# Batch 0's x in head pairs over two load queues, in a fused cross-attention and SiLU feed-forward kernel

## The chip, the core and the metric

The kernel runs on one core of a Trainium2 chip. The metric is the device time of one execution in microseconds (us). The core's engines run side by side and wait for one another through semaphores: TensorE (PE for matmuls, PEld for loading their weights), VectorE (DVE), ScalarE (ACT), GpSimd (POOL) and SyncE (SP). SP, ACT and POOL can issue DMA transfers, each on a queue of its own; in the profile SP's is q1, ACT's is q10 and POOL's is q0. Matmuls write to PSUM, which the kernel divides into eight banks; all else lies in SBUF.

## The reference

There are 8 batches, 8 heads, 512 tokens, 32 state rows and a head width of 64. Tokens attend to the state rows and state rows to the tokens; the two results are concatenated and go through a feed-forward layer with SiLU. Cut to what matters:

```python
scores = scale * np.matmul(x, state.transpose(0, 1, 3, 2))
a = np.exp(scores - scores.max(-1, keepdims=True))
a /= a.sum(-1, keepdims=True) + 1e-09
xread = np.matmul(a, state)
# sread: the same with the state as queries, and x as keys and values
attn = np.concatenate([xread, sread], axis=2)        # (8, 8, 544, 64)
x2 = attn.transpose(0, 2, 1, 3).reshape(8 * 544, 512)
h = x2 @ w_in                                        # (4352, 2048)
out = (h * (1.0 / (1.0 + np.exp(-h)))) @ w_out
```

The last line is `silu(h) @ w_out`; the softmax is over the 32 state rows for xread.

## The kernel before

All matmuls take bf16 operands and sum in f32. The kernel never forms xread. For each batch it multiplies the state with `w_in` once (`W1`, 256 rows by 2048), so that h comes from the softmax weights: `h = W1^T aT` (`emit_G1`, line 522), then SiLU on ACT (line 554) gives `g`, and `g` times `w_out` (`G2`, line 563) gives the output. A batch has 16 column tiles of h (`ft`, 128 columns each) and four tiles of 128 tokens (`tt`). State rows' results of all batches are worked off at the end (lines 543 and 585).

The order of the work is written out by hand: each engine runs its instructions in the order in which the program text emits them. A tile in a PSUM bank or SBUF buffer waits for the last reader of the one that held the place before.

What the change touches is the start of the program, batch 0, before the stream of G1 and G2 matmuls.

- **Loads.** ACT's queue loads batch 0's state (line 173), SP's queue loads x of batch 0 in two halves of four heads (line 179). POOL makes the identity matrix and then issues weight loads, which also cast to bf16 (lines 186 to 195). Line 177 is a small activation that makes ACT load its exp table.
- **Warming matmuls.** `keep_busy(n, ...)` runs n matmuls on zeros (line 165), 16 in all before the first real tile of h; their results are not used.
- **State.** The state's rows are cast on DVE, brought into transposed form by four matmuls (line 230), and copied into `stT` by DVE and ACT (lines 261 to 266).
- **x.** `cast_x` casts x to bf16 (lines 259, 260, 269, 270, 272: DVE, ACT and POOL share the two halves). `pe_transpose_x` transposes four heads (two pairs) at a time on TensorE (line 252), and DVE or ACT copies the result out of PSUM into `xT`. A pair is two heads, one above the other in the 128 partitions. POOL's cast at line 270 comes behind the loads that it issues.
- **Scores to weights.** `scores` (line 305) multiplies a pair's `xT` with `stT`; `exps` (line 319) takes exponentials on ACT; `norm` sums them on DVE (line 378), takes reciprocals (379) and multiplies (381) on POOL for the first four heads, and on DVE for the others. The results `an` are transposed on TensorE (line 397) into `aT`.
- **W1 of batch 0.** Its first 128 columns come from line 616, 384 more from lines 632 to 648, with matmuls on small tiles (line 468); the rest follows in the loop.
- **The first batch's loop** (lines 654 to 686). For each ft, `upto` emits tiles of h ahead of their use by `LEAD0[ft]`, `W0` says at which ft 512 further columns of batch 0's W1 are made, `W1_AT` at which ft a piece of batch 1's, and `T3` fits in the fourth token tile. `place_one_state` at ft 1 places batch 1's state.

In the profile all casts and copies stand under the lines of the helper `copy`: 157 on ACT, 159 on DVE and POOL. The tiles' names tell them apart: `x_rows<-x_f` is a cast of x, `xT<-ps_xt` a copy of transposed x, `aT<-ps_at` of transposed softmax weights, `W<-ps_w` of a piece of W1.

PSUM tiles of h rotate through two buffers, `psH`; `bank` hands out four others in turn.

Of the kernel before, what the change touches and what calls it, by code (L numbers as in the profile page):

```python
# [8 lines left out]
FP32 = mybir.dt.float32  # L9
# [33 lines left out]
def kernel(  # L43
# [105 lines left out]
    def load_w_in(f, n=512):  # L149
        nc.gpsimd.dma_start(w_in_sb[:, :, ds(f, n)], win_re[:, :, ds(f, n)])  # L150
# [4 lines left out]
    def copy(eng, dst, src):  # L155
        if eng is nc.scalar:
            nc.scalar.activation(dst, src, func=COPY, bias=0.0)  # L157
        else:
            eng.tensor_copy(dst, src)  # L159


    def keep_busy(n, pool, tag):
        ps = pool.tile([128, 512], FP32, tag=tag, name="ps_busy")
        for _ in range(n):
            nc.tensor.matmul(  # L165
                ps[:], busy[:, 0:128], busy[:], start=True, stop=True, skip_group_check=True
            )
# [7 lines left out]
        state[0].rearrange("h (m v) d -> (h m) (v d)", v=2),  # L175
    )
    nc.scalar.activation(warm[:], busy[:, 0:1], func=EXP, bias=0.0)
    for hg in range(2):
        nc.sync.dma_start(
            x_f[0][:, ds(4 * hg, 4), :, :],  # L180
            x[0, ds(4 * hg, 4)].rearrange("h (p c) d -> p h c d", p=128, c=4),
        )
    nc.vector.memset(stT[:, 0], 0.0)
    nc.vector.memset(stT[:, 1:8], 0.0)
    make_identity(nc, ident)
    load_w_in(0, 128)
    load_w_in(128, 384)
    load_w_out(0, 2)
# [32 lines left out]
            for v in range(2):  # L221
                copy(eng, by_n[:, :, 0:3:2, :, v], ps[ds(64 * v, 64), :, :, u, :])

    keep_busy(7, psH, "h1")
    copy(nc.vector, st0_n[:], st0_f[:])
    ps0 = bank([128, 4, 16, 2], FP32, "ps_st0")
    by_head = ident.rearrange("p (k u m) -> p k u m", u=2, m=16)
    for v in range(2):
        for u in range(2):
# [6 lines left out]
                tile_position=(0, 64 * u),  # L236
                skip_group_check=True,
            )
    keep_busy(2, psH, "h1")

# [3 lines left out]
    def pe_transpose_x(b, hg, nb=2, new=bank, engs=(nc.vector, nc.scalar), only=None):  # L244
        if b not in xT:
            xT[b] = xtpool.tile([128, 4, 4, 128], BF16, tag="xT", name=f"xT{b}")
        m = 4 // nb
        for u in range(nb) if only is None else only:
            ps = new([128, m, 2, 128], BF16, "ps_xt")
            for i in range(m):  # L250
                for j in range(2):
                    nc.tensor.transpose(  # L252
                        ps[:, i, j, :],
                        x_nat[b][:, m * u + i, 2 * hg + j, :],
                        ident[:],
                    )
            copy(engs[u], xT[b][:, ds(m * u, m), ds(2 * hg, 2), :], ps[:])

    cast_x(0, nc.vector, 0, 2, 0, 4)
    cast_x(0, nc.scalar, 2, 2, 0, 4)  # L260
    for u in range(2):
        copy(
            both[u],
            slots_of(0)[u].rearrange("p g (k n) -> p g k n", n=NS)[:, :, 0:3:2, :],
            ps0[ds(64 * u, 64)].rearrange("p (g k) m v -> p g k (m v)", g=2),
        )
    o_tags = ["o0", "o1"]
    new_o = lambda sh, dt, nm: psO.tile(sh, dt, tag=o_tags.pop(), name=nm)
    cast_x(0, nc.scalar, 2, 2, 4, 4)
    cast_x(0, nc.gpsimd, 0, 1, 4, 4)  # L270
    pe_transpose_x(0, 0, 2, new_o, (nc.vector, nc.vector))
    cast_x(0, nc.vector, 1, 1, 4, 4)

    st_x = pers.tile([128, 8, B, 4, 2, 2], BF16)

# [23 lines left out]
    def scores(b, hg, m=4, new=bank):  # L299
        sc_ps[hg] = []  # L300
        for c in range(4):
            if c % m == 0:
                sc_ps[hg].append(new([128, m, 4, NS], FP32, "ps_sc"))
            for j in range(2):
                nc.tensor.matmul(  # L305
                    sc_ps[hg][-1][:, c % m, ds(2 * j, 2), :],
                    xT[b][:, c, 2 * hg + j, :],
                    stT[:, b, 2 * hg + j, :, :],
                    start=True,
                    stop=True,  # L310
                    skip_group_check=True,
                )

    def exps(b, hg):
        e = epool.tile([128, 4, 4, NS], BF16, tag="exp", name="exp_nat")
        exp_nat[b, hg] = e
        n = 4 // len(sc_ps[hg])
        for i, ps in enumerate(sc_ps[hg]):
            nc.scalar.activation(e[:, ds(n * i, n)], ps[:], func=EXP, bias=0.0, scale=SCALE)  # L319
# [51 lines left out]
    def norm(b, hg, parts=((nc.gpsimd, 0, 4),), nr=4):  # L371
        e = exp_nat[b, hg]
        rs = att.tile([128, 4, 4, 1], FP32, tag="rs", name="rs")
        rc = att.tile([128, 4, 4, 1], FP32, tag="rc", name="rc")
        a = att.tile([128, 4, 4, NS], BF16, tag="an", name="an")
        an[b, hg] = a
        for c in range(0, 4, nr):
            nc.vector.tensor_reduce(rs[:, ds(c, nr)], e[:, ds(c, nr)], axis=AX, op=ADD)
        nc.vector.reciprocal(rc[:], rs[:])
        for eng, c, n in parts:  # L380
            eng.tensor_tensor(  # L381
                a[:, ds(c, n)],
                e[:, ds(c, n)],
                rc[:, ds(c, n)].to_broadcast([128, n, 4, NS]),
                op=MULT,
            )
        if hg == 0:
            aT[b] = att.tile([128, 2, 4, 128], BF16, tag="aT", name="aT")
# [95 lines left out]
    def w1_cols(b, cols, engs, new=bank):  # L484
        w1_out(b, cols, engs, w1_mms(b, cols, new))
# [31 lines left out]
    def g1_half(k, hg):  # L517
        b, ft = divmod(k, NFT)
        if hg == 0:
            pool, tag = (psA, "a1") if k == 1 else (psH, "h1")  # L520
            h_ps[k] = pool.tile([128, 512], FP32, tag=tag, name="h1")
        nc.tensor.matmul(  # L522
            h_ps[k][:],
            W1[b][:, hg, ds(128 * ft, 128)],
            aT[b][:, hg, :, :],
            start=(hg == 0),
            stop=(hg == 1),
            skip_group_check=True,
        )
# [73 lines left out]
            done[0] += 1  # L603

    new_h = lambda sh, dt, nm: psH.tile(sh, dt, tag="h1", name=nm)
    new_o = lambda sh, dt, nm: psO.tile(sh, dt, tag=o_tags.pop(), name=nm)
    keep_busy(1, psH, "h1")
    scores(0, 0)
    exps(0, 0)
    keep_busy(1, psH, "h1")  # L610
    pe_transpose_x(0, 1, 2, new_h, both)
    norm(0, 0)
    scores(0, 1, 2)
    exps(0, 1)
    norm(0, 1, ((nc.vector, 0, 4),), 2)
    w1_cols(0, [(0, 128)], (nc.scalar, nc.scalar))
    nc.scalar.activation(warm[:], busy[:, 0:1], func=SILU, bias=0.0)
    load_w_in(1024)
# [223 lines left out]
```

The softmax here doesn't subtract the row's maximum and nothing guards it: scores larger than these inputs give would overflow.

## Time and profile before

| | |
|---|---|
| median of 4 runs | 213.06 us (212.92 to 213.18) |
| time of the profiled execution | 212.92 us |
| its span, first to last instruction | 211.1 us |
| PE busy | 205.9 us, 97% |
| ACT, DVE, POOL busy | 139.2, 73.8 and 39.6 us |
| mean granted clock of TensorE | 0.997 |
| read from HBM, written | 17.43 MB, 8.91 MB |

The time and the span differ by 1.8 us that lie around the instructions. Engines overlap, so their busy times don't add up. PE's ends of matmuls are modelled: a new matmul starts before the one before it has ended, so where one group of equal matmuls is back to back, the spacing of the starts is its cost. Lines of the timeline read: start, length, engine, source line, operation, output and input with their shapes, how many in a row, and in brackets how long the engine had been idle and for whom it waited. In the views of the DMA traffic each queue stands with its packets, MB and the share of the 16 DMA engines that it took in that window.

### The profile page before, as it was taken

What the parts mean: (1) busy time and instruction counts of PE and PEld (TensorE: products, weight loads), DVE (VectorE), ACT (ScalarE), POOL (GpSimd) and SP (SyncE); (2) the same over time, 40 slices, a digit from 0 to 9 for tenths busy, and PEclk for the clock granted to TensorE, in tenths of its full rate; (3) what the DMA queues carried; (4) which work ended last, traced back from release to release, by engine and by line L of the source; (5) the groups of instructions that cost most, each with busy time, mean ns of one, the idle gap of its engine ahead of it and who ended that gap; (6) DMA issues with size and microseconds to landing.
All of it is one profiled execution on the core that took longest, in us unless ns stands there. A gap on an engine that the chain in (4) does not pass through costs nothing.

```text
span 211.1 us, 3864 instructions
## 1 busy us (share of the span) xinstructions
PE 205.9 (97%) x1575; PEld 96.9 (46%) x1575; DVE 73.8 (35%) x146; ACT 139.2 (66%) x244; POOL 39.6 (19%) x62
## 2 busy tenths in 40 slices
PE   7899999999999999999999999999999999999993
PEld 2443454455444444444444544444444444466653
DVE  3851267657741236113410653043412306100011
ACT  3865677899577867697569855996775166644410
POOL 8691313604220402021201302000200000000000
PEclk9999999999999999999999999999999999999998
DMA  5999999994749555546835628115321111011112
GB/s 190 204 201 207 288 260 350 231 277 159 108 123 267 169 127 126 135 163 106 226 93 175 109 67 200 50 50 102 83 66 43 62 60 53 0 50 50 53 50 99
DMA packets 42929, 28.65 MB, mean 136 GB/s; under 512 B 28064, under 2 KB 37792, under 8 KB 42912
## 3 DMA queue, kind: packets, MB, share of 16 engines
q1 hardware_dynamic: 36720, 20.65, 38.1%
q0 software_dynamic: 5904, 7.64, 17.4%
q8 instruction: 12, 0.20, 0.4%
q10 hardware_dynamic: 288, 0.13, 0.2%
q14 instruction: 5, 0.04, 0.1%
HBM read 17.43 MB, written 8.91 MB: 125 GB/s over the span
## 4 chain that ended last, share of the span: by engine, by line
PE 94%; DMA 3%; ACT 1%; DVE 1%; SPq 0%; issue 0%
PE o L563 51%; PE h L522 26%; PE ps_w L468 4%; PE h L543 3%; PE o_a L563 3%; DMA x_f<-in_x_dram 3%; PE o_part L585 2%; PE ps_sr L415 1%; PE ps_scT L331 1%; PE ps_busy L165 1%; PE ps_sc L305 1%; PE ps_at L397 0%; PE ps_xt L252 0%; DVE W L159 0%; ACT x_rows L157 0%; ACT exp_nat L319 0%
## 5 line engine op out<-in xcount | busy, mean ns | idle before, releaser
L563 PE MATMUL o<-w_out_sb,g 128*128 128x512 bf16 x496 | 131.8, 379 | 0.0
L554 ACT ACTIVATE g<-h 128x512 bf16<-128x512 f32 (+1 forms) x143 | 81.3, 573 | 35.3 <-PE h L522 21.2
L563 PEld LDWEIGHTS <-g 128*128 128x128 bf16 x528 | 50.2, 98 | 58.8 <-issue 3.9
L522 PE MATMUL h<-aT,W 128*128 128x512 bf16 x254 | 74.6, 379 | 0.1
L159 DVE COPY o_sb<-o 128x512 f32<-128x512 f32 x15 | 10.4, 691 | 89.6 <-PE o L563 86.1
L522 PEld LDWEIGHTS <-W 128*128 128x128 bf16 x254 | 24.5, 98 | 30.6 <-issue 1.2
L159 DVE CAST W<-ps_w 128x512 bf16<-128x512 f32 (+2 forms) x36 | 22.3, 659 | 23.7 <-PE ps_w L468 23.7
L157 ACT ACTIVATE W<-ps_w 128x512 bf16<-128x512 f32 (+1 forms) x32 | 16.3, 562 | 10.1 <-PE ps_w L468 10.1
L159 POOL CAST x_nat<-x_f 128x512 bf16<-128x512 f32 x24 | 14.2, 633 | 33.8 <-DMA x_f<-in_x_dram 33.8
L157 ACT ACTIVATE o_sb<-o 128x512 f32<-128x512 f32 x16 | 9.6, 597 | 14.3 <-PE o L563 11.8
L361 POOL TENSOR_TENSOR an<-e,rcn 128x512 bf16<-128x512 bf16 x5 | 7.6, 1519 | 50.3 <-DVE rcn L359 50.3
L468 PE MATMUL ps_w<-w_in_sb,stT 64*32 64x512 bf16 (+2 forms) x264 | 10.2, 374 | 0.0
L563 PE MATMUL o_a<-w_out_sb,g 128*128 128x512 bf16 x32 | 10.0, 379 | 0.0
L543 PE MATMUL h<-xmT,w_in_sb 128*128 128x256 bf16 x64 | 9.6, 273 | 0.0
L543 PEld LDWEIGHTS <-w_in_sb 128*128 128x128 bf16 x64 | 6.3, 98 | 3.9
L165 PE MATMUL ps_busy<-busy 128*128 128x512 bf16 x16 | 6.2, 506 | 1.2 <-DVE warm L172 1.2
L358 DVE TENSOR_REDUCE rs<-e 128x32 f32<-128x1024 bf16 x5 | 6.1, 1213 | 3.2 <-DMA e<-eT 3.2
L345 ACT ACTIVATE eT<-ps_scT 128x512 bf16<-128x512 f32 x10 | 5.4, 594 | 1.6 <-PE ps_scT L331 1.6
L784 ACT ACT_TABLE_LOAD x5 | 6.4, 1283 | 0.1
L381 POOL TENSOR_TENSOR an<-exp_nat,rc 128x512 bf16<-128x512 bf16 x3 | 3.1, 1049 | 14.6 <-ACT eT L345 9.4
L468 PEld LDWEIGHTS <-stT 64*32 64x32 bf16 x264 | 3.2, 90 | 5.5 <-issue 4.2
L766 ACT ACT_TABLE_LOAD x4 | 5.1, 1283 | 0.1
(76 smaller groups left out, 99.6 us busy)
## 6 DMA issues: line engine op xcount, KB each, us to landing
out_dram<-o_sb SPq DMA_DIRECT2D x33, 256.0 KB, 2.7
x_f<-in_x_dram SPq DMA_DIRECT2D x4, 1024.0 KB, 6.1
x_f<-in_x_dram POOLq DMA_DIRECT2D x2, 1024.0 KB, 12.1
w_in_sb<-in_moe_w_in_dram POOLq DMA_DIRECT2D x3, 512.0 KB, 10.4
x_f<-in_x_dram SPq DMA_DIRECT2D x2, 512.0 KB, 4.8
w_out_sb<-in_moe_w_out_dram POOLq DMA_DIRECT2D x4, 256.0 KB, 12.0
w_out_sb<-in_moe_w_out_dram POOLq DMA_DIRECT2D x2, 512.0 KB, 12.3
x_f<-in_x_dram POOLq DMA_DIRECT2D x2, 512.0 KB, 15.2
```

Source lines behind the costliest of these rows:

```text
L157: nc.scalar.activation(dst, src, func=COPY, bias=0.0)
L159: eng.tensor_copy(dst, src)
L165: nc.tensor.matmul(ps[:], busy[:, 0:128], busy[:], start=True, stop=True, skip_group_check=True)
L345: nc.scalar.activation(t[:, hg], scT_ps[hg][:], func=EXP, bias=0.0, scale=SCALE)
L358: nc.vector.tensor_reduce(rs[:], e2[b][:], axis=AX, op=ADD)
L361: eng.tensor_tensor(a[:, hg], e2[b][:, hg], rc[:, hg].to_broadcast([128, 4, 4, NS]), op=MULT)
L468: nc.tensor.matmul(pss[f, hg][ds(32 * s, 32), 0:n], stT[ds(r, 64), b, h // 2, s % 2, :], w_in_sb[ds(r, 64), h // 2, ds(f, n)], start=True, ...
L522: nc.tensor.matmul(h_ps[k][:], W1[b][:, hg, ds(128 * ft, 128)], aT[b][:, hg, :, :], start=(hg == 0), stop=(hg == 1), skip_group_check=True,)
L543: nc.tensor.matmul(ps[:, 0:256], w_in_sb[:, kt, ds(128 * ft, 128)], xmT[:, :, kt].rearrange("p t n b -> p t (n b)"), start=(kt == 0), stop ...
L554: nc.scalar.activation(g[:, 0:n], ps[:, 0:n], func=SILU, bias=0.0)
L563: nc.tensor.matmul(outs[tt][:], gt[b * NFT + ft][:, ds(128 * tt, 128)], w_out_sb[:, ft, :], start=(ft == 0), stop=(ft == NFT - 1), skip_gr ...
L784: nc.scalar.activation(warm[:], busy[:, 0:1], func=SILU, bias=0.0)
```

## The change

It has six parts.

1. x of batch 0 is loaded by four transfers of one pair (two heads, 256 KB) each: pairs 0 and 1 on SP's queue, pairs 2 and 3 on ACT's, after the activation that loads the exp table.
2. POOL writes the ones beside x in the first `x_rows` buffer (two memsets) before its first weight load, and no longer after the last ones.
3. Three warming matmuls less (7 to 6, 2 to 1, and one of those between the transposes).
4. Casts, transposes, scores and exponentials go by pairs. Casts: pair 0 on DVE, pair 1 on ACT, pair 2 on DVE, pair 3 half on ACT and half on POOL. All four copies of transposed x are DVE's. Scores of pairs 0 and 1 share a PSUM bank and one exponential; pairs 2 and 3 have one each.
5. The products of normalising are halves: both of the first four heads on POOL, and of the others one on DVE and one on POOL; all sums and reciprocals stand behind the last copy of xT on DVE.
6. In the first batch's loop, the first 512 columns of batch 1's W1 move from ft 4 to ft 2, beside those of batch 0; the lead at ft 1 is 3 and not 2; tiles 4 and 5 of h go to `bank` and not to `psH`.

```diff
-    for hg in range(2):
-        nc.sync.dma_start(
-            x_f[0][:, ds(4 * hg, 4), :, :],
-            x[0, ds(4 * hg, 4)].rearrange("h (p c) d -> p h c d", p=128, c=4),
-        )
+    for k in range(4):
+        load_x(0, 2 * k, 2, nc.sync if k < 2 else nc.scalar)
...
     make_identity(nc, ident)
+    ones_beside_x(0, nc.gpsimd)
     load_w_in(0, 128)
...
-    keep_busy(7, psH, "h1")
+    keep_busy(6, psH, "h1")
...
-    keep_busy(2, psH, "h1")
+    keep_busy(1, psH, "h1")
...
-    cast_x(0, nc.vector, 0, 2, 0, 4)
-    cast_x(0, nc.scalar, 2, 2, 0, 4)
+    cast_x(0, nc.vector, 0, 4, 0, 2)
...
-    cast_x(0, nc.scalar, 2, 2, 4, 4)
-    cast_x(0, nc.gpsimd, 0, 1, 4, 4)
-    pe_transpose_x(0, 0, 2, new_o, (nc.vector, nc.vector))
-    cast_x(0, nc.vector, 1, 1, 4, 4)
+    cast_x(0, nc.scalar, 0, 4, 2, 2)
+    cast_x(0, nc.gpsimd, 2, 2, 6, 2)
...
-            pool, tag = (psA, "a1") if k == 1 else (psH, "h1")
-            h_ps[k] = pool.tile([128, 512], FP32, tag=tag, name="h1")
+            if k == 1:
+                h_ps[k] = psA.tile([128, 512], FP32, tag="a1", name="h1")
+            else:
+                h_ps[k] = (bank if k in IN_BANKS else new_h)([128, 512], FP32, "h1")
...
+    IN_BANKS = (4, 5)
...
+    def pair_xT(k, new):
+        ps = new([128, 4, 128], BF16, "ps_xt")
+        for c in range(4):
+            nc.tensor.transpose(ps[:, c, :], x_nat[0][:, c, k, :], ident[:])
+        copy(nc.vector, xT[0][:, :, k, :], ps[:])
+
+    def pair_scores(k, ps):
+        for c in range(4):
+            nc.tensor.matmul(
+                ps[:, c],
+                xT[0][:, c, k, :],
+                stT[:, 0, k, :, :],
...
-    keep_busy(1, psH, "h1")
-    scores(0, 0)
-    exps(0, 0)
-    keep_busy(1, psH, "h1")
-    pe_transpose_x(0, 1, 2, new_h, both)
-    norm(0, 0)
-    scores(0, 1, 2)
-    exps(0, 1)
-    norm(0, 1, ((nc.vector, 0, 4),), 2)
+    ps_sc0 = bank([128, 4, 4, NS], FP32, "ps_sc")
+    pair_xT(0, new_o)
+    keep_busy(1, psH, "h1")
+    cast_x(0, nc.vector, 0, 4, 4, 2)
+    pair_xT(1, new_o)
+    pair_scores(0, ps_sc0[:, :, 0:2, :])
+    pair_xT(2, new_h)
+    pair_scores(1, ps_sc0[:, :, 2:4, :])
+    cast_x(0, nc.scalar, 0, 2, 6, 2)
+    nc.scalar.activation(e0[0][:], ps_sc0[:], func=EXP, bias=0.0, scale=SCALE)
+    for k in (2, 3):
+        if k == 3:
+            pair_xT(3, new_h)
+        ps = bank([128, 4, 2, NS], FP32, "ps_sc")
+        pair_scores(k, ps)
+        nc.scalar.activation(
+            e0[1][:, :, ds(2 * k - 4, 2), :], ps[:], func=EXP, bias=0.0, scale=SCALE
+        )
...
+    for hg in range(2):
...
+        for s, n in ((0, 4),) if hg == 0 else ((0, 2), (2, 2)):
+            nc.vector.tensor_reduce(
+                rs0[hg][:, :, ds(s, n)], e0[hg][:, :, ds(s, n), :], axis=AX, op=ADD
+            )
+        nc.vector.reciprocal(rc0[hg][:], rs0[hg][:])
+        for c in (0, 2):
+            (nc.vector if hg == 1 and c == 0 else nc.gpsimd).tensor_tensor(
+                an[0, hg][:, ds(c, 2)],
+                e0[hg][:, ds(c, 2)],
+                rc0[hg][:, ds(c, 2)].to_broadcast([128, 2, 4, NS]),
+                op=MULT,
+            )
...
-    for i in range(3):
+    for i in (1, 2):
         ones_beside_x(i, nc.gpsimd)
...
-    W1_AT = {4: 0, 6: 512}
-    LEAD0 = [2, 2, 2, 2, 2, 3, 2, 1, 3, 3, 2, 3]
+    W1_AT = {2: 0, 6: 512}
+    LEAD0 = [2, 3, 2, 2, 2, 3, 2, 1, 3, 3, 2, 3]
...
-        elif ft in W1_AT:
-            w1_cols(1, [(W1_AT[ft], 512)], both)
```

More of the change, by code (lines that the diff above doesn't have):

```diff
@@ L266 @@
         )
-    o_tags = ["o0", "o1"]
-    new_o = lambda sh, dt, nm: psO.tile(sh, dt, tag=o_tags.pop(), name=nm)
-    cast_x(0, nc.scalar, 2, 2, 4, 4)
-    cast_x(0, nc.gpsimd, 0, 1, 4, 4)
-    pe_transpose_x(0, 0, 2, new_o, (nc.vector, nc.vector))
-    cast_x(0, nc.vector, 1, 1, 4, 4)
+    cast_x(0, nc.scalar, 0, 4, 2, 2)
+    cast_x(0, nc.gpsimd, 2, 2, 6, 2)
     st_x = pers.tile([128, 8, B, 4, 2, 2], BF16)
@@ L605 @@
     new_h = lambda sh, dt, nm: psH.tile(sh, dt, tag="h1", name=nm)
+    IN_BANKS = (4, 5)
+    o_tags = ["o0", "o1"]
     new_o = lambda sh, dt, nm: psO.tile(sh, dt, tag=o_tags.pop(), name=nm)
-    keep_busy(1, psH, "h1")
-    scores(0, 0)
-    exps(0, 0)
-    keep_busy(1, psH, "h1")
-    pe_transpose_x(0, 1, 2, new_h, both)
-    norm(0, 0)
-    scores(0, 1, 2)
-    exps(0, 1)
-    norm(0, 1, ((nc.vector, 0, 4),), 2)
+    xT[0] = xtpool.tile([128, 4, 4, 128], BF16, tag="xT", name="xT0")
+    aT[0] = att.tile([128, 2, 4, 128], BF16, tag="aT", name="aT")
@@ new lines, in pair_xT @@
+    def pair_xT(k, new):
[9 more added lines that the diff above has]
+                stT[:, 0, k, :, :],
+                start=True,
+                stop=True,
+                skip_group_check=True,
+            )
@@ new lines @@
+    e0 = [epool.tile([128, 4, 4, NS], BF16, tag="exp", name="exp_nat") for _ in range(2)]
+    for hg in range(2):
+        exp_nat[0, hg] = e0[hg]
+    ps_sc0 = bank([128, 4, 4, NS], FP32, "ps_sc")
+    pair_xT(0, new_o)
+    keep_busy(1, psH, "h1")
+    cast_x(0, nc.vector, 0, 4, 4, 2)
[5 more added lines that the diff above has]
+    nc.scalar.activation(e0[0][:], ps_sc0[:], func=EXP, bias=0.0, scale=SCALE)
@@ new lines @@
+    for k in (2, 3):
[6 more added lines that the diff above has]
+        )
+    rs0, rc0, a0 = {}, {}, {}
+    for hg in range(2):
+        rs0[hg] = att.tile([128, 4, 4, 1], FP32, tag="rs", name="rs")
+        rc0[hg] = att.tile([128, 4, 4, 1], FP32, tag="rc", name="rc")
+        an[0, hg] = att.tile([128, 4, 4, NS], BF16, tag="an", name="an")
+        for s, n in ((0, 4),) if hg == 0 else ((0, 2), (2, 2)):
[9 more added lines that the diff above has]
+                op=MULT,
+            )
```

## The prediction

> **What bounds the kernel now.** I read the page first, then the chain of waits for the first 13 us, then the timeline of that stretch engine by engine, then DMA traffic in short windows.
>
> The page's busy line and the chain's split by engine:
>
> ```profile
> PE 205.9 (97%) x1575; PEld 96.9 (46%) x1575; DVE 73.8 (35%) x146; ACT 139.2 (66%) x244; POOL 39.6 (19%) x62
> PE 94%; DMA 3%; ACT 1%; DVE 1%; SPq 0%; issue 0%
> ```
>
> TensorE sets the time. The other 6% is the start, where batch 0 has to become scores before TensorE has real work. The chain there (start, length, what):
>
> ```profile
> 1.27 5.32 DMA x_f<-in_x_dram
> ...
> 6.61 0.63 ACT x_rows L157
> ...
> 7.27 0.60 ACT exp_nat L319
> 7.87 0.58 ACT xT L157
> ...
> 8.49 0.29 PE ps_sc L305 x4
> ...
> 11.39 0.49 PE h L506 x3
> 11.88 0.52 PE h L522 x2
> ```
>
> The second half of x lands at 6.59; cast, scores, exponentials, normalising and transposes follow, and the last matmul of the first h tile (third of the "x3", starts 0.11 apart) starts at 11.61. From there matmuls follow one another at 0.216 us for 512 columns; between 11.8 and 50 us the spacings hold only one stall near 0.22 us, one near 0.16 us and small ones. So the time moves by the shift of that 11.61, plus whatever the edits behind it save. The rows that I use for the shift:
>
> ```profile
> 5.83 0.75 POOL L153 DMA_DIRECT2D w_out_sb<-in_moe_w_out_dram  x1
> ...
> 6.64 0.40 POOL L159 CAST x_rows<-x_f 128x256 bf16<-128x256 f32 x1
> ...
> 7.61 0.42 DVE L159 COPY xT<-ps_xt 128x512 bf16<-128x512 bf16 x1 [0.42 <-PE ps_xt L252]
> ...
> 7.95 0.68 DVE L378 TENSOR_REDUCE rs<-exp_nat 128x16 f32<-128x512 bf16 x1
> ...
> 9.07 1.05 POOL L381 TENSOR_TENSOR an<-exp_nat,rc 128x512 bf16<-128x512 bf16 x1 [2.03 <-DVE rc L379]
> ```
>
> POOL casts only after its last early DMA issue. And the first reduction on DVE runs between copies of xT, while TensorE and ACT still work on the other heads.
>
> **The change part by part.**
>
> *Loads of x.* Two issues of 512 KB on SP become four of 256 KB: pairs 0 and 1 on SP, 2 and 3 on ACT. An issue takes 0.42 (ACT's state load) to 0.48 us (SP), so SP ends at 1.7 as now. ACT's two stand behind the first table load (1.20 to 2.48) in the program; later in this trace the records of ACT's sequencer have a semaphore wait of line 345 at 92.80, ahead of the table load at 93.41 that precedes it in the program, so I let the two issue at 1.2 and 1.7, before the first byte of x moves (2.0). Then both queues share. In the window 2.73 to 3.25:
>
> ```profile
> q1 hardware_dynamic: 119, 0.12, 66.3%
> q10 hardware_dynamic: 70, 0.03, 22.3%
> ```
>
> SP's q1 and ACT's q10 (state) went side by side. Packets of both up to 2.73, 3.25, 4.2 and 5.07 us are 129, 318, 670 and 1005, one KB each for x; q1 alone had 55, 174, 526 and 861. With equal turns from 2.73, SP has sent pair 0 (256 packets) at 129+2x201 = 531, that is at 3.83, and pair 1 (512) at 129+2x457 = 1043, at 5.2. The first half now reached 512 plus its completions at about 4.2 and landed at 5.09, 0.87 later. So pair 0 lands at 4.7, pair 1 at 6.1, pair 2 near 5.3, pair 3 at 6.4 to 6.6. Pair 1, worked second, comes third. Ends: 5.1 (pair 1 in the place of the first half now) and 6.59 (as late as the second half now). I take 6.1, from the shared window.
>
> A rule of the Trainium skill speaks against two queues: "DMA: Bandwidth & Descriptors", section "Issuing engines are not separate DMA queues", says that loads from several issuers interleave on the same 16 DMA engines and save only issue time. The rates of 372 and 383 GB/s from 3.25 to 5.07 on one queue agree. By the rule taken strictly pair 1 would gain nothing over 6.59, and the sum below would end at +1.1 in place of +0.6.
>
> *Weights later.* The two memsets of x_rows (0.33 and 0.13 us, overlapping to 0.30) move from 21.94 on POOL to before the first weight load: POOL's seven early issues and its cast move by 0.30 to 0.46; I take 0.4. No packet of q0 (weights) moves before 5.07, when x has 861 of 1056 packets out, so x gains little: 0 to 0.4 us at its last packets, and only pair 3 could use it. Weights lose 0 to 0.46; the first use is TensorE's at 8.71 (landed at 7.07) and 9.64 (landed at 9.32), both behind what moves more. Leaving POOL at 21.94 saves nothing: it waits for other things there.
>
> *The cast of pair 3 on POOL* (columns 2 and 3) now stands at 6.64+0.4 = 7.04 and ends at 7.44, whenever pair 3 lands before 7.0. Transposes of pair 3 cannot start before 7.5. That is a floor.
>
> *The staircase of pairs.* DVE and ACT run in program order. With pair 1 at 6.1: ACT casts it 6.12 to 6.75 (0.63). TensorE's transposes 6.80 to 6.97 (four, 0.056 apart); DVE's copy starts 0.26 after the last, as now (7.36 to 7.61), 7.23 to 7.65. Pair 2's transposes follow pair 0's scores, and its copy runs at 7.61 to 8.03; pair 2's scores at 8.09 to 8.18; only then pair 3's transposes (8.21 to 8.38), copy 8.64 to 9.06. Now one copy of xT runs on ACT beside DVE's; in the change all four are DVE's, and the third and fourth wait for each other through TensorE. DVE then does in a row what partly overlapped: reduction 0.68 and reciprocal 0.25 for the first four heads (to 9.94), two reductions of 0.42 and a reciprocal (to 10.96), a product of about 0.42 (half of 0.70 plus the fixed part). POOL does three half products, 0.53 each by half of 1.05: 10.10 to 11.16, and the last 11.16 to 11.70. DVE's product ends at 11.4, so POOL's is last. Transposes 11.75 and 11.81, copy 0.26 later for 0.29, last matmul of the first h at 12.42: +0.81. ACT (exponentials 0.60 and two of 0.38, W copies 0.44, table load 1.28) is through at about 11.6, in time. Hidden: the cast of pair 0 and of pair 2 (0.43 each) in DVE's wait for pair 1. The sequence moves one for one with pair 1: neutral at 5.3, +1.3 at 6.59, and not below about 0 because of POOL's floor (-0.25 if POOL's halves take less and DVE's path decides).
>
> *Fewer warming matmuls*, 16 to 13: they lie in waits, save nothing; whether the clock notices is a rival. Earlier start of the state's matmuls (one busy matmul less, 0.4 us at 4.28) is covered by the wait for pair 0.
>
> *Batch 1's first W1 piece from ft 4 to ft 2, lead and banks.* The rows show two visits to the small tiles now and one joined visit:
>
> ```profile
> 14.97 0.41 PE L468 MATMUL ps_w<-w_in_sb,stT 64*32 64x512 bf16 x8
> ...
> 18.03 0.41 PE L468 MATMUL ps_w<-w_in_sb,stT 64*32 64x512 bf16 x8
> ```
>
> Each entry and each exit costs 0.09 to 0.10 us over the column time (14.67 to 14.97, 15.00 to 15.32). One visit less saves 0.19. Its needs: batch 1's state placed by DVE (14.53 now, with the piece at about 15.2), both psH buffers free (SILU of the early fourth h ends some 0.6 us before), and the h of tiles 4 and 5 in other banks. The wait that could replace it costs 0 to 0.2; I keep -0.19.
>
> *Sum.* +0.81 - 0.19 = +0.62 on the profiled execution: 212.92 (span 211.1) to 213.54. The median of the runs is 0.14 higher, 213.06, so 213.7.
>
> **The rivals.**
>
> *Pairs land in their order* (ends at or below the time before). If ACT's loads wait behind the table load, they issue at 2.7 and 3.2, SP has the engines alone and pair 1 lands at about 5.1. For: they stand behind it in ACT's program. Against: the wait passed at 92.80. Pair 1 no longer decides; POOL's floor does: 0 to -0.25, with -0.19: -0.2 to -0.45, 212.6 to 212.9. It decides from pair 1 before about 5.3. Chance 0.22.
>
> *Weights become late.* Only if the start does not slip: w_in for tile 4 lands at 14.63 and is used at 14.97, w_out for ft 4 lands at 18.14 and is used at 18.37. A full 0.46 with an unmoved start gives 0.2 to 0.45 of stall, less 0.19: 213.1 to 213.3. Against: bytes that x leaves earlier are free for weights. Chance 0.08.
>
> *The clock comes later.* Warming matmuls start 0.43 apart up to 3.72 and 0.22 apart from 8.89:
>
> ```profile
> 1.19 3.17 PE L165 MATMUL ps_busy<-busy 128*128 128x512 bf16 x7 [1.19 <-DVE warm L172]
> ...
> 8.89 0.82 PE L165 MATMUL ps_busy<-busy 128*128 128x512 bf16 x3
> ```
>
> At half rate four transposes take 0.16 longer, three times in series, and the scores as much again; if it lasts past 11.6 each 512-column matmul loses 0.21. So +0.5 to +1.3 on top of +0.62: 214.2 to 215.0. For: TensorE's streaming up to 5.1 falls by about 0.4 us. Against: it still has six, four and one matmuls. The page "TensorE: Matmul & The Clock Gate" (Part 1) gives a free-running window of about 3.4 us for the switch; no row here shows the window. Chance 0.13.
>
> *x no faster and pair 1 last* is the late end of the forecast (+1.1, 214.2), and belongs to its range.
>
> **How the numbers follow.** Forecast 0.52, with its own range +0.25 to +1.1 (213.3 to 214.2); the rivals as above; 0.05 for none of these. Without the page's reading the late end stands from the row of 6.59. The range that leaves out 2 in 10 goes from 212.6, the in-order case, to 214.7 inside the late clock. A measurement of this kernel tells about 0.2% (0.43 us) from no change. Slower: 0.42 of the forecast, the clock's 0.13, 0.03 of the rest, 0.58. Faster: 0.10 of the in-order case and 0.02 of the rest, 0.12. Within: 0.30.
>
> **What would show it.** Pair 1's cast on ACT near 6.1 and not 5.1; POOL's cast near 7.0; DVE's four xT copies ending near 9.1 with three reductions after it; POOL's last product ending near 11.7; the last of the four first h matmuls near 12.4; one visit of 16 small-tile matmuls at ft 2 and none at ft 4. I am wrong if pair 1 lands by 5.3, if POOL's halves are much shorter than 0.53, if the transposes start 0.11 apart after 6 us, or if a stall appears at ft 2.

## The result and the profile after

| | before | after |
|---|---|---|
| median | 213.16 us (61 runs, 212.82 to 214.47) | 213.97 us (41 runs, 213.14 to 216.28) |
| ratio of the runs' means | | 1.0048, interval 1.0035 to 1.006 |
| profiled execution, its span | 212.92, 211.1 | 213.82, 212.1 |

The changed kernel is slower, by half a per cent in the mean and 0.4% in the median (ratios here are always of means), and its runs spread: 17 of the 41 lie at 213.50 or below, 8 between 213.79 and 214.32, 16 at 214.79 or above. Before, one run of 61 lies above 213.5. So there are two questions: what the typical loss is, and what makes the spread.

The page after the change, busy line and split of the chain:

```profile
PE 204.9 (97%) x1572; PEld 96.7 (46%) x1572; DVE 74.0 (35%) x147; ACT 138.5 (65%) x243; POOL 41.1 (19%) x64
PE 93%; DMA 4%; POOL 1%; DVE 1%; issue 0%; POOLq 0%
```

TensorE has a little less to do than before (205.9) and the span is longer, so the loss is waiting. The chain's share of the transfers went from 3% to 4%, and what is transferred has changed. The chain of waits up to 13 us (start, length, what):

```profile
1.31 0.26 POOL x_rows L115
1.56 0.05 POOL x_rows L118
1.61 0.87 POOL w_in_sb L150
2.48 8.41 DMA w_in_sb<-in_moe_w_in_dram
...
10.93 0.36 PE ps_w L461 x8
...
12.32 0.71 PE h L499 x4
```

Before, x headed this chain (5.32 us of transfer). Now it is the second piece of `w_in`, issued at 2.48 and landed at 10.89 (before 9.32). The last matmul of the first h tile (the fourth of "PE h L499") starts at 12.76, against 11.61: 1.15 us later. From that start to the end of the span it is 199.3 us, against 199.5 before: nearly the whole difference lies in the first 13 us, and the loop gives a little back.

The timeline of the same stretch (start, length, engine, line, operation, idle time before and for whom):

```profile
5.55 0.63 ACT L157 ACTIVATE x_rows<-x_f 128x512 bf16<-128x512 f32 x1 [0.16 <-DMA x_f<-in_x_dram]
...
6.75 0.40 POOL L159 CAST x_rows<-x_f 128x256 bf16<-128x256 f32 x1
...
8.05 0.42 DVE L159 COPY xT<-ps_xt 128x512 bf16<-128x512 bf16 x1 [0.61 <-PE ps_xt L610]
8.39 0.68 DVE L651 TENSOR_REDUCE rs<-exp_nat 128x16 f32<-128x512 bf16 x1
...
9.50 1.95 POOL L656 TENSOR_TENSOR an<-exp_nat,rc 128x256 bf16<-128x256 bf16 x3 [2.36 <-ACT W L157]
...
10.27 0.70 DVE L656 TENSOR_TENSOR an<-exp_nat,rc 128x256 bf16<-128x256 bf16 x1
...
10.93 0.36 PE L461 MATMUL ps_w<-w_in_sb,stT 64*32 64x384 bf16 x8 [1.03 <-DMA w_in_sb<-in_moe_w_in_dram]
...
16.23 0.63 PE L461 MATMUL ps_w<-w_in_sb,stT 64*32 64x512 bf16 x16
```

The reader sees two delays that lie beside each other. The staircase: DVE's fourth copy ends at 8.47, the reduction follows, and POOL's three half products end at 11.45, where its one product ended at 10.12. And the weights: TensorE has nothing to do from 9.90 and waits 1.03 us for the piece of `w_in`. The last line is the joined visit to the small tiles, 16 matmuls in a row.

The two delays can be told apart. In three later profiles of the same staircase in which no weights are waited for last (given below), the last h matmul starts 0.72 to 0.73 after POOL's last product ends (11.31 and 12.03, 11.85 and 12.58, 11.94 and 12.66). By the staircase alone it would be 11.45 + 0.72 = 12.17, 0.56 later than before; the remaining 0.59 is the weights'.

How x left the queues, in three windows one after the other, 2.73 to 3.50, 3.50 to 4.30 and 4.30 to 5.07 us (packets, MB, share of the 16 DMA engines):

```profile
q1 hardware_dynamic: 242, 0.24, 88.3%
q10 hardware_dynamic: 67, 0.03, 13.4%
...
q1 hardware_dynamic: 235, 0.23, 81.7%
q10 hardware_dynamic: 72, 0.07, 25.9%
...
q10 hardware_dynamic: 253, 0.24, 91.4%
q1 hardware_dynamic: 57, 0.04, 16.8%
```

SP's queue q1 had most of the engines until 4.3, then ACT's q10. The pairs landed at 4.37, 5.47, 5.88 and 6.61, in their order.

And how the weights moved. After 6.2 no packet of x is left in either kernel, and POOL's q0 is alone on the engines. From 6.2 to 7.2, 7.2 to 8.2 and 8.2 to 9.2 it moved 0.18, 0.20 and 0.20 MB before the change, and 0.15, 0.17 and 0.14 MB after it. The third of these stretches, first before, then after (a share above 100% means that packets overlap in time):

```profile
q0 software_dynamic: 224, 0.20, 125.0%
...
q0 software_dynamic: 173, 0.14, 118.1%
```

The 512 packets of the second piece of `w_in` (768 bytes each) begin at 5.81 before and 6.09 after, 0.28 later, but the last one begins at 8.91 and 10.52, 1.61 later. So most of its delay arises when x is already out, at a lower rate of the weights. Why the rate falls no run shows.

### The profile page after: what moved, and what is told of

It is laid out like the page before. It is cut to its first block, busy times and chain, and to the rows that moved or that the text cites. A ratio compares the mean times of both kernels' runs of the same rounds, so it can differ in the third digit from the quotient of the medians.

```text
span 212.1 us, 3868 instructions
## 1 busy us (share of the span) xinstructions
PE 204.9 (97%) x1572; PEld 96.7 (46%) x1572; DVE 74.0 (35%) x147; ACT 138.5 (65%) x243; POOL 41.1 (19%) x64
## 3 DMA queue, kind: packets, MB, share of 16 engines
HBM read 17.43 MB, written 8.91 MB: 124 GB/s over the span
## 4 chain that ended last, share of the span: by engine, by line
PE 93%; DMA 4%; POOL 1%; DVE 1%; issue 0%; POOLq 0%
PE o L558 51%; PE h L517 26%; DMA w_in_sb<-in_moe_w_in_dram 4%; PE ps_w L461 4%; PE h L538 3%; PE o_a L558 3%; PE o_part L580 2%; PE ps_sr L408 1%; PE ps_scT L324 1%; PE ps_sc L298 0%; PE ps_xt L250 0%; POOL w_in_sb L150 0%; PE h L499 0%; DVE W L159 0%; PE ps_at L390 0%; PE ps_busy L165 0%
## 5 line engine op out<-in xcount | busy, mean ns | idle before, releaser
L159 POOL CAST x_nat<-x_f 128x512 bf16<-128x512 f32 x24 | 14.8, 659 | 34.8 <-issue 34.0
L165 PE MATMUL ps_busy<-busy 128*128 128x512 bf16 x13 | 5.1, 510 | 1.2 <-DVE warm L172 1.2
L109 POOL DMA_DIRECT2D x_f<-in_x_dram x4 | 3.3, 841 | 9.3 <-DVE x_rows L159 7.0
```

The lines of the kernel that those rows point to most:

```text
L165: nc.tensor.matmul(ps[:], busy[:, 0:128], busy[:], start=True, stop=True, skip_group_check=True)
```

## The experiments

Three readings of the late weights were open at first: that the third queue (ACT's) is what slows them, that POOL's later start does, or that the order does in which loads of x and of weights are issued. Beside them stood the clock: fewer warming matmuls, and so a late full clock. In the expectations R stands for the third queue, P for POOL's later start, O for the order of issues and C for the clock. The runs came in three groups, each on one chip and beside runs of the kernel before (medians 213.0, 213.0 and 213.1).

### The ones back at their old place

```diff
-    ones_beside_x(0, nc.gpsimd)
     load_w_in(0, 128)
...
-    for i in (1, 2):
+    for i in range(3):
         ones_beside_x(i, nc.gpsimd)
```

> The changed kernel with the ones of the first x_rows buffer written where they were, after the last loads, so that POOL issues the first weight load 0.12 us earlier (at 1.43). Theory P: the 384 columns land near 9.4 and the median falls to 213.3. Theory R: nothing moves by more than 0.15 us; median 213.8 to 214.1.

Measured: 213.70 (213.06 to 214.88), ratio 1.0048 (1.003 to 1.0066): the same as the whole change, and not the 213.3 of theory P. Its profiled execution was the fastest, 213.06, with weights on time (the second piece of `w_in` landed at 9.36), so it stands for the best case and not for the median. Its timeline shows the staircase without the other delay:

```profile
7.02 0.40 POOL L159 CAST x_rows<-x_f 128x256 bf16<-128x256 f32 x1 [0.47 <-DMA x_f<-in_x_dram]
...
9.36 1.95 POOL L655 TENSOR_TENSOR an<-exp_nat,rc 128x256 bf16<-128x256 bf16 x3 [1.94 <-ACT W L157]
9.54 0.36 PE L460 MATMUL ps_w<-w_in_sb,stT 64*32 64x384 bf16 x8
...
11.48 0.81 PE L498 MATMUL h<-aT,W 128*128 128x256 bf16 x4
```

The last h matmul starts at 12.03, 0.72 after POOL's end at 11.31: the staircase costs 0.42, the loop gives 0.2 back, and the span is 211.3 against 211.1. The place of the ones is not what costs the median; POOL's first weight issue moves by 0.12 us only (1.43 to 1.55).

### All four pair loads on SP, and then the weights issued after them

```diff
-        load_x(0, 2 * k, 2, nc.sync if k < 2 else nc.scalar)
+        load_x(0, 2 * k, 2, nc.sync)
```

> The changed kernel, but all four pair loads of x on SP's queue. Theory R (the third queue in use is what makes the first weights late): the weight load of 128 columns lands near 7.2 us and that of 384 columns near 9.5 (8.86 and 10.89 in the changed kernel), TensorE does not wait for the latter, and the time falls to 213.0 to 213.4 with the runs close together. Theory P (weights are late because POOL starts them later): they land as late as in the changed kernel and the median stays near 214.0. Theory S (my staircase of pairs sets the start whatever the weights do): the last matmul of the first h still starts near 12.2 against 11.6 before, and about 0.4 us of loss remains, 213.5.

Measured: 217.07 (216.59 to 218.38), ratio 1.02 (1.0179 to 1.0222), much slower, with no x on ACT's queue at all. None of the forecasts (213.0 to 214.0) came near. Part of it is TensorE's clock, which in the profile was granted at half from 8.41 to 15.24 us. The chain of waits:

```profile
1.76 0.47 SPq L109
2.23 0.04 issue
2.27 7.97 DMA x_f<-in_x_dram
10.24 0.02 issue
10.26 0.42 ACT x_rows L157
```

Pairs 0 and 1 landed at 4.05 and 4.77, but pair 2 at 7.38 and pair 3 at 10.24. Their issues stand at 1.76 and 2.27, behind POOL's first weight issue at 1.55. The next kernel keeps SP's four loads and lets POOL write all three buffers of ones and a scratch tile first, so that the first weight issue comes at 3.05:

```diff
-    ones_beside_x(0, nc.gpsimd)
+    for i in range(3):
+        ones_beside_x(i, nc.gpsimd)
+    idle = pers.tile([128, 1024], BF16)
+    nc.gpsimd.memset(idle[:], 0.0)
     load_w_in(0, 128)
```

> As the first experiment (four pair loads on SP), but POOL writes all three buffers of ones and a scratch tile of 1024 columns before its first weight load, which so starts near 3.0 us, after SP's fourth issue at 2.27. Theory O (a load of x that is issued after the first weight load has begun shares the DMA engines with the weights and is stretched): the four pairs now land in order near 4.0, 4.8, 5.6 and 6.4, where they landed at 4.05, 4.77, 7.38 and 10.24; TensorE keeps the full clock from about 5 us on, and the time falls from 217 to 213.5 to 214.5, although all weights and POOL's cast of pair 3 come about 1.5 us later. Theory N (the third and fourth transfer on a queue are slow by themselves): pair 3 still lands after 8 us and the time stays above 216.

Measured: 215.72 (214.89 to 216.0). The pairs landed at 4.09, 4.80, 5.54 and 6.34, 0.7 to 0.8 apart, as theory O foresaw. Beside POOL's memsets nothing but the order of the issues differs, so these two profiles show it: a load of x issued after the first load of weights is stretched, by 1.8 us for pair 2 and 3.9 us for pair 3. The time fell by 1.35 us and missed the 213.5 to 214.5 expected: POOL's cast of pair 3 now stands behind its late issues, and the full clock, against the expectation, was lost again from 9.34 to 12.75 us. Its timeline:

```profile
6.36 0.42 ACT L157 ACTIVATE x_rows<-x_f 128x256 bf16<-128x256 f32 x1 [0.60 <-DMA x_f<-in_x_dram]
...
8.30 0.45 POOL L159 CAST x_rows<-x_f 128x256 bf16<-128x256 f32 x1
```

In the other kernels the first weight issue is POOL's at 1.43 or 1.55; two halves on SP are issued by 1.27, ACT's second pair at 1.77. What their profiles show:

| x of batch 0 | last x landed | second piece of `w_in` landed |
|---|---|---|
| two halves on SP (five kernels) | 6.44 to 6.59 | 9.32, 9.38, 9.68, 9.68, 9.76 |
| a half on each queue | 6.38 | 10.18 |
| pairs over two queues (six kernels) | 6.32 to 8.47 | 9.36, 10.16, 10.45, 10.66, 10.89, 11.04 |
| pairs on SP | 10.24 | 11.68 |

For x the table fits the order of the issues: what is issued ahead of the weights lands by 6.59, what is issued behind them lands as late as 8.47 or 10.24, though not always late. For the weights the order is not enough. With a half on each queue all of x is issued by 1.28, ahead of the weights, and still their second piece lands at 10.18, later than with any halves on SP. Theory R (ACT's queue in use) stays open for the weights, though it can't be the whole, as they land at 11.68 with SP alone and at 9.36 once with ACT's queue in use.

The rule that the prediction quoted from the Trainium skill, "DMA: Bandwidth & Descriptors", section "Issuing engines are not separate DMA queues", that loads of several issuers interleave on the same 16 engines, agrees with the rows: from 5.6 to 6.2 in the changed kernel's profile, POOL's queue (129.7%) and ACT's (18.0%) move packets side by side. Equal turns between the two queues of x, which the prediction had taken, are not in the rows.

### The loads alone in the kernel before

```diff
-    for hg in range(2):
-        nc.sync.dma_start(
...
+    for k in range(4):
+        load_x(0, 2 * k, 2, nc.sync if k < 2 else nc.scalar)
```

> The kernel before with nothing changed but the loads of batch 0's x: four pair loads, two on SP and two on ACT. Theory R: weights land late here too (9.8 to 10.9 for the 384 columns), TensorE waits for them, and the time goes to 213.4 to 214.2 with a wide spread. Theory P: weights land as before (9.3), time 213.1, within 0.1%. If the first half (pairs 0 and 1, both on SP) lands earlier than 5.09, the casts of the first four heads start earlier.

Measured: 213.94 (213.63 to 216.14), ratio 1.0057 (1.0035 to 1.0079). The new loads alone, with the old order of work, cost what the whole change costs. Theory R's numbers came out, but by theory O the weights would be late here too, so the run doesn't tell the two apart. The profiled execution was the slowest (216.14), with pair 3 at 8.47, `w_in` at 11.04, and the clock lost (below).

### The edit of the loop alone

```diff
-    W1_AT = {4: 0, 6: 512}
-    LEAD0 = [2, 2, 2, 2, 2, 3, 2, 1, 3, 3, 2, 3]
+    W1_AT = {2: 0, 6: 512}
+    LEAD0 = [2, 3, 2, 2, 2, 3, 2, 1, 3, 3, 2, 3]
```

(with tiles 4 and 5 of h in `bank`, as in the change)

> The kernel before with the loop's edit alone (batch 1's first W1 piece at ft 2, lead 3 at ft 1, tiles 4 and 5 of h in other banks). My step says one visit to the small tiles less, -0.19 us: ratio 0.9991, about 212.85 where before is 213.05, and no new wait at ft 2. The rival is a wait in its place: ratio 1.000 or above.

Measured: 212.82 (212.6 to 213.07), ratio 0.9993 (0.9984 to 1.0001): 0.15 less in the mean, 0.19 in the median. That is the gain foreseen, at the edge of what can be measured, and it is the lowest median of all kernels here.

### Two halves with the new order of work

In the first, x is loaded in halves on SP as before; in the second, one half on SP and one on ACT.

```diff
-    for k in range(4):
-        load_x(0, 2 * k, 2, nc.sync if k < 2 else nc.scalar)
+    for hg in range(2):
+        load_x(0, 4 * hg, 4, nc.sync)
```

> The changed kernel with the loads of x as before (two halves on SP); casts by pairs, later ones, fewer warming matmuls and the loop's edit stay. Theory O: both halves are issued before the weights (by 1.75), land at 5.1 and 6.6, and the runs lie within 0.6 us of one another; what is left is the staircase (pair 1 at 5.1; last copy of xT ends near 8.3, last matmul of the first h at 12.0 against 11.61) less 0.19 for the loop: 213.2 to 213.4. Theory P or C (weights' start, warming): spread up to 215 as in the changed kernel.

```diff
+    for hg in range(2):
+        load_x(0, 4 * hg, 4, (nc.sync, nc.scalar)[hg])
```

> The changed kernel with x in two halves, one on SP (heads 0 to 3, issued at 0.74) and one on ACT (issued at 1.27). Theory O: both issues precede the first weight load at 1.55, so x lands by 6.6 and the time is as with two halves on SP, 213.2 to 213.5, close together. Theory R (a third queue in use is the cause): weights late, spread as in the changed kernel, median near 214.0.

Measured: 215.49 (214.54 to 215.54) and 215.47 (214.56 to 215.62), ratio 1.0108 for both (1.0092 to 1.0124). The expectation of a small loss fell. With SP's halves the loads were as wanted, x at 5.02 and 6.46, `w_in` at 9.38; with a half on each queue x landed at 4.93 and 6.38, and `w_in` at 10.18. What cost the time is in TensorE's timeline of the first:

```profile
5.60 0.61 PE L610 MATMUL ps_xt<-ident,x_rows 128*128 128x128 bf16 x4 [0.60 <-DVE x_rows L159]
...
8.73 0.61 PE L610 MATMUL ps_xt<-ident,x_rows 128*128 128x128 bf16 x4
...
13.10 0.86 PE L390 MATMUL ps_at<-ident,an 128*128 128x128 bf16 x8
```

The changed kernel's profile has for the same four transposes of pair 0:

```profile
4.96 0.40 PE L610 MATMUL ps_xt<-ident,x_rows 128*128 128x128 bf16 x4
```

They take 0.61 in the one and 0.40 in the other (starts 0.107 apart and 0.056). TensorE ran at half speed up to 13.6 us; the records of the granted clock begin only there. (The view's column for the clock shows 1.00 before the first grant, and the mean clock of a run leaves that time out; the spacing of the matmuls tells.) So theory C came to the fore: the spread is the clock's.

The clock's records, in every profile, are cut in steps of 3.413 us: the changed kernel's full clock lasts 61 of them, the kernel before's 60, that of the halves 59, and in the run of the loads alone one step full and one half come first. So I took TensorE's busy time in the steps before and after each grant (ahead of the first grant there is no record, and the steps are counted back from it). Halves on SP, grant at 13.61:

```profile
3.37:6.78 3.41, 2.59 (x13) 1.00 1.18 290
6.78:10.20 3.42, 2.66 (x33) 1.00 1.26 198
10.20:13.61 3.41, 3.07 (x27) 1.00 1.27 204
```

The loads alone in the kernel before, granted at 7.19, half from 10.60 to 14.01, then full:

```profile
3.78:7.19 3.41, 3.41 (x21) 1.00 1.10 233
7.19:10.60 3.41, 1.55 (x24) 1.00 1.25 188
10.60:14.01 3.41, 3.41 (x29) 0.50 1.27 203
```

The two steps nearest to the limit, one of the half on each queue, not followed by a grant, and one of the weights behind SP's four loads, followed by one:

```profile
2.88:6.29 3.41, 2.79 (x13) 1.00 1.16 318
...
9.34:12.75 3.41, 2.80 (x24) 0.50 1.25 192
```

(The columns are the stretch, its length, PE's busy time as the view models it with the number of matmuls, the clock, the share of the DMA engines and GB/s.) In the 14 profiles of all kernels the clock was granted after every step with 2.80 us busy or more (lowest 2.80, 2.83, 2.90), not granted after steps of 2.79, 2.66, 2.61, 2.59 and 1.10, taken back after 1.55, 1.60 and 1.64, and kept after 1.97 and more. Busy times hold modelled ends of matmuls, so the limit is about 2.8 us here and no sharper. The page "TensorE: Matmul & The Clock Gate" of the Trainium skill (Part 1) describes a free-running activity window of about 3.4 us; these steps agree with it.

### The waits of TensorE filled

Theory C was put to the test by filling gaps with warming matmuls and taking them out where they were.

```diff
-    keep_busy(6, psH, "h1")
+    keep_busy(7, psH, "h1")
...
-    keep_busy(1, psH, "h1")
+    keep_busy(2, psH, "h1")
...
     pair_xT(0, new_o)
-    keep_busy(1, psH, "h1")
+    keep_busy(2, psH, "h1")
...
             pair_xT(3, new_h)
+            keep_busy(2, psH, "h1")
```

> The changed kernel with five warming matmuls more, all of them in stretches where TensorE waits: 7 and 2 at the start as before the change, 2 and not 1 after the transposes of pair 0, 2 between the transposes and the scores of pair 3. Theory C (clock): the profiles show full clock granted and taken back in steps of 3.413 us, and the changed kernel leaves TensorE idle for 0.67 us after pair 0's transposes and 0.52 us before pair 3's scores; where a step falls over them, the grant comes late, and this makes the spread of 213.1 to 216.3. Filled, no run lies above 214.3 and the median is 213.2 to 213.6. Rival W (the spread comes from the order in which x and the weights reach the transfer engines, which differs from run to run): nothing changes, median near 214.0, a third of the runs at 214.8 or more. Rival S (the additional matmuls stand in the path): above 214.0 in all runs.

Measured: 213.62, all seven runs within 213.58 to 213.91, ratio 1.0029 (1.0018 to 1.004). The tail is gone, as theory C had it, with the median 0.02 above its range; so are the runs below 213.5. An earlier run had filled only the first two places:

> The changed kernel with two of the three warming matmuls given back (7 and 2 instead of 6 and 1). Theory C (some executions get the full clock a window later, since the start is less busy): the mean granted clock is 0.997 or more in every run and the runs above 214.2 us with a clock of 0.982 to 0.992 go away; median 213.4 to 213.9. Theory R: the spread stays, since most of the late runs of the changed kernel have a clock of 1.0; median near 214.0.

Measured: 213.61 (213.08 to 214.97, one of nine runs above 214.1), ratio 1.0031 (1.0015 to 1.0048). The tail is shorter with two matmuls and gone with five; the one late run has a mean granted clock of 0.990.

The same filling in the kernel with two halves on SP:

> The changed kernel with x loaded in two halves on SP as before (215.49 in its run) and with the five warming matmuls more. Theory C: the 215.49 was the clock granted at 13 us; filled, the median falls to 213.2 to 213.6, since x lands at 5.0 and 6.5, the weights are on time, and only the staircase is left. Rival (halves that land late cost this much through the staircase's chain of casts and copies): 215.0 or more, as without the filling.

Measured: 213.75 (213.70 to 213.90), ratio 1.0031 (1.0019 to 1.0043), where it was 215.49 unfilled, though on another chip. That is 0.15 above the range expected and far from the rival's 215.0. Five matmuls on zeros are worth 1.7 us here. Its timeline shows the staircase alone, with x in halves:

```profile
9.99 1.95 POOL L657 TENSOR_TENSOR an<-exp_nat,rc 128x256 bf16<-128x256 bf16 x3 [2.82 <-ACT W L157]
...
10.18 0.36 PE L461 MATMUL ps_w<-w_in_sb,stT 64*32 64x384 bf16 x8
...
12.12 0.81 PE L499 MATMUL h<-aT,W 128*128 128x256 bf16 x4
```

No wait for weights, full clock from 5.56, and POOL's products end at 11.94, 1.8 us later than the one product before. The last h matmul starts at 12.66.

And filled with the ones at their old place:

> The changed kernel with the ones written at their old place and the five warming matmuls more. Theory C together with late weights: 213.1 to 213.4, 0.1 to 0.4 below the filled kernel with the ones first, since the wait for the second piece of w_in (1.03 us in the changed kernel's profile, none in the profile with the ones late) is the other thing that TensorE waits for. Rival (the place of the ones is of no account): the same median as the filled kernel within 0.1. If the staircase alone is left, the median is 0.42 less 0.15 above before: 213.3.

Measured: 213.71 (213.62 to 213.91), ratio 1.0031 (1.0019 to 1.0043), 0.1 above the filled kernel with the ones first and not 0.1 to 0.4 below. The expectation fell and its rival holds: where the ones are written makes no difference of more than 0.1. The profile shows why: the weights were late here too.

```profile
9.20 1.95 POOL L656 TENSOR_TENSOR an<-exp_nat,rc 128x256 bf16<-128x256 bf16 x3 [2.14 <-ACT W L157]
...
10.49 0.36 PE L460 MATMUL ps_w<-w_in_sb,stT 64*32 64x384 bf16 x8 [0.92 <-DMA w_in_sb<-in_moe_w_in_dram]
...
11.88 0.71 PE L498 MATMUL h<-aT,W 128*128 128x256 bf16 x4
```

With the same loads and the same place of the ones, `w_in` landed at 9.36 in one profile and at 10.45 in this; and in the filled kernel with the ones first pair 3 landed at 7.52:

```profile
8.01 0.40 PE L610 MATMUL ps_xt<-ident,x_rows 128*128 128x128 bf16 x4 [0.37 <-ACT x_rows L157]
...
10.70 0.36 PE L461 MATMUL ps_w<-w_in_sb,stT 64*32 64x384 bf16 x8 [0.55 <-DMA w_in_sb<-in_moe_w_in_dram]
...
12.09 0.76 PE L499 MATMUL h<-aT,W 128*128 128x256 bf16 x4
```

In the six profiles with pairs over two queues the last x and the second piece of `w_in` land at 6.32 and 10.45, 6.61 and 10.89, 6.97 and 9.36, 6.97 and 10.16, 7.52 and 10.66, 8.47 and 11.04: one of the two is always late, sometimes both. What decides it from one execution to the next no run shows.

Open is why no filled run reaches the 213.1 to 213.5 of the changed kernel's best ones; all three filled profiles have a late transfer or late halves, but three profiles can't show that every run has. The additional matmuls don't stand in the path behind DVE's fourth copy: from its end to the end of POOL's last product it takes 2.98 in the three filled profiles (8.87 to 11.85, 8.96 to 11.94, 8.16 to 11.14) as in the changed kernel's (8.47 to 11.45).

### Fewer warming matmuls in the kernel before

```diff
-    keep_busy(7, psH, "h1")
+    keep_busy(6, psH, "h1")
...
-    keep_busy(2, psH, "h1")
+    keep_busy(1, psH, "h1")
...
     exps(0, 0)
-    keep_busy(1, psH, "h1")
```

> The kernel before with only part 3 of the change: 13 warming matmuls (6, 1, and none between the first exponential and the transposes of the other heads). Theory C: TensorE then streams without a gap only from 1.2 to about 5.0 us, so full clock is granted late in some executions: some runs at 214.0 to 215.5 beside others at 212.9 to 213.3, the median at 213.2 or more. Rival (the number of warming matmuls is of no account, as the prediction took it): all runs 212.8 to 213.5, median 213.0.

Measured: 213.47 (212.85 to 215.18, 12 runs), ratio 1.0033 (1.001 to 1.0056). Three runs lie at 215.12 to 215.18, the others at 212.85 to 213.62, with nothing between. So part 3 by itself brings a tail, in 3 runs of 12, and the rival that the number is of no account fell. That the clock came late in these three is taken from theory C: the profiled execution is one of the quick ones (213.00, granted at 4.02), and none of the three left a trace.

## Why the prediction was right, and where not

The predicted 213.7 lies 0.27 below the median of 213.97, inside the range; the direction was right. Its steps:

- **Loads of x: the step "both queues share" failed.** Taken was equal turns from 2.73, with pairs at 4.7, 6.1, 5.3 and 6.4 to 6.6. Measured: SP's queue had 82 to 88% up to 4.3, and the pairs came at 4.37, 5.47, 5.88 and 6.61. That ACT's loads issue ahead of the end of the table load was right (1.28 and 1.77). The rival "pairs land in their order" had the order right, its reason wrong, and its gain did not come, for the next two points.
- **Weights later: mis-sized, and its cover was no cover.** 0 to 0.46 was foreseen, hidden behind what moves more. The two first pieces landed 1.79 and 1.57 later, and TensorE waited 1.03, worth 0.59 at the end of the start. The working asked only how late POOL begins (0.12 and not 0.30 to 0.46), so that by its figures ACT's second load of x (1.7) came ahead of the first weight load (1.43 and 0.4); in fact it is issued behind it (1.77 and 1.55). And it took the weights' rate as given, which fell from 0.58 to 0.45 MB between 6.2 and 9.2. The cause of that is open. The rival "weights become late" looked for the stall at tile 4; there it is 0.11 (16.23).
- **The staircase: mechanism right.** Four copies on DVE, the third and fourth waiting for each other through TensorE, POOL's product last. The fourth copy ended at 8.47 and not 9.06, as pair 1 came 0.63 earlier. The halves were mis-sized: 0.53 each by half of 1.05, but three took 1.95 and not 1.60, and DVE's half took 0.70 and not 0.42. So POOL ended at 11.45 and not 11.70: two misses of 0.59 and 0.35 in opposite directions. From there to the last h matmul the working's 0.72 is right to 0.01 where no weights are awaited.
- **Cast of pair 3 on POOL:** foreseen at 7.04, it started at 6.75, as POOL's issues moved by 0.12 and not by 0.4.
- **Fewer warming matmuls "save nothing", and the late clock had 0.13.** Too little. 16 of 41 runs lie at 214.79 or above, where the rival put them (214.2 to 215.0, in fact up to 216.3), and taking out the same number before the change brings a tail in 3 of 12. Its argument against, "it still has six, four and one matmuls", counted matmuls and not the idle time between them.
- **The loop:** -0.19 foreseen, 0.15 measured, with the one visit of 16.
- **The sum:** +0.62 on the profiled execution, measured +0.90: staircase +0.56 (foreseen +0.81), weights +0.59 (0), loop about -0.2 (-0.19). That the size came out is in part luck. The working lets the staircase move one for one with pair 1, which landed 0.63 before the 6.1 taken; by that alone the sum would have been about 0. POOL's longer halves and the late weights, which the sum had at too little and at nothing, made up for it.

Split by cause the mean stands so: filled, that is without the tail, the change costs 0.29% (ratio 1.0029, median 213.62 against 213.1); this is the staircase and the transfers less the loop's gain, and whatever the filling itself costs, which was not measured by itself. The rest up to 0.48% is the tail's. That the tail is the clock's is shown for other kernels, by the profiles of the halves and by the filling. In the changed kernel itself the mean granted clock is 0.992 or less in 9 of the 41 runs, all at 214.25 or above, 7 of them in the tail; the other 9 runs of the tail read 0.999 or 1.0, as a late first grant would, but none of them was profiled. The old order with pair loads (213.94) and the new order with halves (213.75, filled) both lose, so neither the loads nor the new order pays by itself here.

## What to carry to other kernels

When loads of one tensor are split, look at when each issue stands against the first issue of the next tensor: a load of x issued behind the first load of weights landed 1.8 and 3.9 us later here than one issued ahead of it. Warming matmuls in waits are not free to remove: count the busy time of TensorE in every stretch as long as the clock's step, in any position, before and after the edit. Half of an elementwise operation must be priced from a row of its own size and its neighbours, not by halving.

## What was not expected of the hardware

- Full clock was granted by steps of 3.413 us: after a step with about 2.8 us of TensorE busy or more (lowest 2.80), and not after one with less (highest 2.79); it was taken back after 1.64 or less. So some 0.6 us of idle time in a step decided whether the next 3.4 us ran at half speed. The position of the steps differs from profile to profile: the first grant came between 4.02 and 7.19 us in twelve of the 14, and at 13.12 and 13.61 in the two kernels with x in halves and no filling.
- POOL's queue, alone on the DMA engines from 6.2 to 9.2 us, moved 0.58 MB in the kernel before and 0.45 MB in the changed one.
- DVE's product of 128x256 took 0.70 us, and DVE's of 128x512 in the kernel before 0.70 at the shortest (0.88 and 0.91 at its other places); POOL's halves took 0.62, 0.61 and, beside DVE's, 0.79, where one whole took 1.05. Whether the two engines hinder each other was not tried.
